# Attention scores in strips of 32 queries, with the mask added by TensorE, and two units to a visit

## The chip, the cores and the metric

One core of one Trainium2 chip. The metric is the device time of one execution in microseconds (us); lower is better. Six engines matter: TensorE (PE in the profile; its weight loads are PEld), VectorE (DVE), ScalarE (ACT), GpSimd (POOL) and SyncE (SP), which issues the transfers. PSUM, where TensorE writes, has eight banks of 2 KB a partition.

## The reference

A windowed attention feeds a maxout FFN. q, k and v are 8 batches x 8 heads x 576 positions x 64, in fp32. The first four heads attend to the last 32 positions (plain), the others to every fourth of the last 128 (dilated).

```python
scores = scale * np.matmul(q, k.transpose(0, 1, 3, 2))
mask_plain = (rel >= 0) & (rel < window)                                  # window = 32
mask_dil = (rel >= 0) & (rel < window * dilation) & (rel % dilation == 0) # dilation = 4
scores = np.where(masks[None, :, :, :], scores, -1000000000.0)
scores = scores - np.max(scores, axis=-1, keepdims=True)
attn = np.exp(scores)
attn = attn / (np.sum(attn, axis=-1, keepdims=True) + 1e-09)
x = np.matmul(attn, v)               # then heads side by side: 4608 tokens x 512
h = np.maximum(np.maximum(x @ w1, x @ w2), x @ w3)    # w1, w2, w3: 512 x 768
return (h @ w_out).astype(np.float32)                 # w_out: 768 x 512
```

## The kernel before

**Units.** Attention is cut into 64 units: 16 halves of 288 positions, times 4 pairs of heads (`half, p = divmod(u, NPAIR)`; pairs 0 and 1 are plain, 2 and 3 dilated). The host lays the dilated heads out by residue, so that their window, too, is 32 neighbouring keys. A plain unit has 3 blocks of 96 queries, each against 128 keys; a dilated one 4 blocks of 72 queries against 104 keys. In either, query i of a block needs the keys from i + 1 to i + 32, counted in the block's keys: a band. The first half of a batch has 32 keys fewer in its first block (plain) or in all (dilated).

**Two ways to do a unit.** Units 0 to 11 (`LEAN`) go through `dense`: TensorE first puts the mask into a bank (identity times `masks`, bf16), adds the scores of both heads, VectorE takes the maxima of a head pair or of one head in one instruction, and TensorE transposes the exponentials. Units 12 to 63 go through `attention` and `behind`, which the change replaces:

- `scores` (line 834): per block and head j one fp32 matmul into `banks[j]`, 96 or 72 queries wide. The two heads use different halves of the array's rows (`kb.t[64j : 64j + 64]`).
- `masked` (line 866): per block and head one `tensor_tensor_reduce` on VectorE; it reads the bank, adds the mask, scales by -0.125, writes into `W` and gives the row minima (`mx`).
- `expo` (line 857): per block and head one ScalarE exponential with the minima as bias; it also gives the row sums (`sm`).
- `clear` (line 892): in first halves GpSimd zeroes the columns of `W` that no key stands for.
- `eps`, `recip` (line 907), `norm` (in the helper `tt`, line 439; VectorE or GpSimd, as the plan decides): the sums become factors, and `W` is multiplied, one instruction a head.
- `turn` (line 928): six VectorE transposes of 32 x 32 squares, for all blocks at once, into `PT`. Only the squares of the band are moved: for query strip i the key strips i and i + 1; the rest of `PT` stays zero.
- `values` (line 940): per block and head an fp32 matmul of `PT` with v into one bank; both heads use different columns of the array. A copy moves it to `raw` (or to `xa`).

**Visits.** TensorE leaves the FFN for one step at a time (`products`): the value products of units whose `PT` is ready, and then scores of later ones. Units 12 to 21 (`TAKEN` = 22) come in pairs, the others one by one, each time with one unit kept in between.

**FFN.** The first 1152 tokens go in three tiles of 384 (`ffn`, lines 1006 and 1059; operands split into a high and a low part, three products). The other 3456 go in four passes of 864, where `combine` prepares sums and differences of token halves (tiles t), `multiplied` multiplies them by prepared weights (line 1306, `wm` from DRAM copies `wS`), and line 1448 multiplies by w_out. In these passes two banks are held for running sums, so that four of the six `b` banks (three couples) are left to attention.

**What sets the order.** Every operation is a step in `Plan`. `deadlines` gives each a due time, back from the FFN, with paces and slacks (`UNIT_PACE`, `UNIT_SLACK`, `COMBINE_SLACK` and others); `order` plays the steps through on a model of the engines and issues them as they come out. Steps with two or three engines in `costs` may move between them. The model's prices and slacks are constants at the top. Before the first FFN step, filler matmuls (line 1551) are put where TensorE would idle. The engines work through their queues in the issued order.

Of the kernel before, what the change touches and what calls it, by code (L numbers as in the profile page):

```python
# [8 lines left out]
F32 = mybir.dt.float32  # L9
# [9 lines left out]
WIN, DIL = 32, 4  # L19
# [10 lines left out]
SHARED = 1.0  # L30
# [5 lines left out]
TAKEN = 22  # L36
# [10 lines left out]
SPILL = 0.065  # L47
MARGIN, MARGIN_FROM = 0.2, 120.0
TO_PE = 0.26
FFN_PACE = 1.044  # L50
UNIT_PACE, UNIT_SLACK, UNIT_LEAD = 1.559, 3.648, 2.329
FILL = 0.22
BURSTS, BURST = (21, 35), 16
WEIGHT_PACE, WEIGHT_SLACK, WEIGHT_LEAD = 0.437, 1.028, 1.545


def blocks_of(hf, dil):

    nb, nq, wk = (4, 72, 104) if dil else (3, 96, 128)
    step, out = (104 if dil else 96), []  # L60
    for i in range(nb):

        mo = WIN if not hf and (dil or i == 0) else 0
        out.append((nq * i, nq, HALF + step * i + mo, wk - mo, mo))
    return out
# [40 lines left out]
class Step:  # L106


    def __init__(self, costs, fn, bufs, nbytes, rows, kind, lead):
# [6 lines left out]
        self.ready = dict.fromkeys(costs, 0.0)  # L116


class Plan:
# [54 lines left out]
    def room(self, st, slots):  # L174
# [6 lines left out]
        for tag in set(new):  # L181
            k = new.count(tag)
            if any(b.width == 2 for b in st.bufs if b.tag == tag and b.slot is None):
                assert k == 1
                at = max(at, self.couple(slots[tag])[0])
            else:
                at = max(at, sorted(slots[tag])[k - 1][0] if len(slots[tag]) >= k else 1e9)
# [11 lines left out]


    def order(self, fill=None):
# [11 lines left out]
        order = []  # L213
        fills, must, bursts = 0, 0, list(BURSTS)
        while len(order) - fills < len(self.steps):
# [43 lines left out]
            for b in st.bufs:  # L259
# [11 lines left out]
            else:  # L271
# [11 lines left out]
                elif e == "dve" and "pool" in st.costs:  # L283
                    both = min(cost, max(0.0, free["pool"] - at))
                    cost += SHARED * both
                    free["pool"] += 0.5 * SHARED * both
                end = free[e] = at + cost
            st.eng = e
# [8 lines left out]
            for n in st.next:  # L297
                n.left -= 1
                for o in n.costs:
                    if e == o:  # L300
                        lat = 0.0 if e == "pe" else 0.03
                    else:
                        lat = self.AFTER[e] + (TO_PE if o == "pe" else 0.0)
                        if n.kind != "ffn" and end > MARGIN_FROM:
                            lat += MARGIN
                    n.ready[o] = max(n.ready[o], end + lat)
# [1305 lines left out]
```

## Time and profile before

| what | value |
|---|---|
| median of 3 runs (lowest to highest) | 741.37 us (740.05 to 741.79) |
| the profiled execution / its span | 739.52 us / 737.7 us |
| granted TensorE clock | full in all slices |
| transfers | 140.16 MB in 83803 packets, 190 GB/s over the span |
| HBM read / written | 113.25 MB / 25.95 MB |

The profile is of one execution. Busy times of engines overlap each other; a matmul's record runs from its start to a modelled end, so that neighbouring records overlap and the distance between starts is the better price. "idle before" is the time an engine stood still ahead of a group, with what released it. `L866` is line 866. A number behind a tile is left out: `banks` stands for all six `b` banks.

### The profile page before, as it was taken

The page shows a single profiled execution, that of the slowest core. Times are in us where ns is not written, and L with a number is a line of the kernel's source. Part 1 is how long each engine was busy: PE and PEld are TensorE (multiplying, and loading weights), DVE is VectorE, ACT ScalarE, POOL GpSimd, SP SyncE. Part 2 cuts the span into 40 slices and gives each one's busy share as a digit, 9 for nine tenths or more (in the row PEclk, how much of TensorE's full clock was granted, in tenths as well). Part 3 has the DMA queues.
Part 4 walks back from the last instruction along what each step waited for, and adds up shares of the span by engine and source line. Part 5 has one row for each costly group of instructions (what it writes and reads, how often), then busy time and mean ns, then how long its engine had stood idle before and what let it go on. Part 6 is the DMA issues. An engine that isn't in the chain of part 4 may idle for free.

```text
span 737.7 us, 14575 instructions
## 1 busy us (share of the span) xinstructions
PE 710.3 (96%) x4880; PEld 612.7 (83%) x4880; DVE 551.2 (75%) x1645; ACT 327.7 (44%) x1136; POOL 314.1 (43%) x388
## 2 busy tenths in 40 slices
PE   7989999989999899999999999999999999999998
PEld 4659888978988788888788899778888877999986
DVE  7988887889878887789867797897788897134241
ACT  4676634424435554445444344545444543222211
POOL 3789457665756411217751122772112185001040
PEclk9999999999999999999999999999999999999999
DMA  9899635246633487876357778435787641677611
GB/s 317 282 340 391 217 103 178 92 144 202 217 113 105 126 239 230 242 232 187 103 170 241 233 228 249 144 113 167 229 239 211 189 131 59 183 223 223 209 43 54
DMA packets 83803, 140.16 MB, mean 190 GB/s; under 512 B 7952, under 2 KB 32272, under 8 KB 83728
## 3 DMA queue, kind: packets, MB, share of 16 engines
q1 hardware_dynamic: 83728, 139.23, 60.5%
q8 instruction: 39, 0.64, 0.4%
q14 instruction: 36, 0.29, 0.1%
HBM read 113.25 MB, written 25.95 MB: 189 GB/s over the span
## 4 chain that ended last, share of the span: by engine, by line
PE 71%; DVE 16%; DMA 5%; POOL 3%; issue 2%; ACT 2%; SPq 0%; DVEq 0%; ACTq 0%; POOLq 0%
PE banks L1306 20%; PE bank L1306 14%; PE bank L1448 14%; PE bank L1006 8%; PE banks L834 5%; DVE PT L928 4%; PE banks L940 4%; DVE tmps L439 3%; DVE W L439 3%; DVE W L866 2%; PE bank L1551 2%; DMA wS<-wu 2%; DVE hx L439 2%; DMA st<-in_w_dn_dram 2%; DMA wS<-tmps 1%
## 5 line engine op out<-in xcount | busy, mean ns | idle before, releaser
L1306 PE MATMUL banks<-t,wm 128*128 128x432 f32 x864 | 188.0, 363 | 3.5 <-DVE mx L866 1.6
L1306 PEld LDWEIGHTS banks<-t,wm 128*128 128x128 f32 x864 | 159.7, 188 | 18.1 <-ACT banks L432 3.0
L857 ACT ACTIVATE W<-W,mx 96x128 f32<-96x128 f32 (+3 forms) x364 | 135.2, 373 | 61.4 <-DVE mx L866 59.6
L1306 PE MATMUL bank<-t,wm 128*128 128x432 f32 x648 | 141.1, 361 | 0.6 <-POOL t L439 0.6
L928 DVE STREAM_TRANSPOSE PT<-W 32x192 f32<-32x192 f32 (+1 forms) x312 | 125.1, 401 | 9.1 <-POOL W L439 3.9
L1306 PEld LDWEIGHTS bank<-t,wm 128*128 128x128 f32 x648 | 120.8, 188 | 8.2 <-POOL t L439 1.0
L1006 PE MATMUL bank<-xa,wu 128*128 128x384 f32 x648 | 119.1, 338 | 2.6 <-ACT xa L432 1.8
L1448 PE MATMUL bank<-wdn,h 128*128 128x512 f32 (+1 forms) x504 | 119.6, 394 | 1.3 <-DVE h L439 0.5
L1006 PEld LDWEIGHTS bank<-xa,wu 128*128 128x128 f32 x648 | 111.5, 188 | 5.8 <-ACT xa L432 2.1
L1448 PEld LDWEIGHTS bank<-wdn,h 128*128 128x128 f32 (+1 forms) x504 | 91.9, 184 | 25.3 <-DVE h L439 1.1
L866 DVE CUSTOM_DVE_ANT_0 W<-banks,masks 96x128 f32<-96x128 f32 (+3 forms) x364 | 76.5, 256 | 38.0 <-PE banks L1306 13.5
L439 POOL TENSOR_TENSOR W<-W,sm 96x384 f32<-96x384 f32 (+4 forms) x56 | 58.5, 1047 | 64.0 <-DVE sm L907 62.5
L902 POOL TENSOR_TENSOR sm<-sm,small_c 96x6 f32<-96x6 f32 (+1 forms) x52 | 14.7, 283 | 134.7 <-ACT W L857 127.7
L857 ACT ACTIVATION_READ_ACCUMULATOR W<-W,mx 72x1 f32 (+1 forms) x364 | 68.6, 188 | 0.0
L432 ACT COPY tmps<-bank 128x432 f32<-128x432 f32 (+1 forms) x47 | 23.7, 504 | 78.1 <-PE bank L1306 63.8
L434 POOL TENSOR_SCALAR h<-hx 128x256 fp32r<-128x256 f32 (+1 forms) x25 | 11.1, 455 | 102.0 <-DVE hx L439 95.9
L439 DVE TENSOR_TENSOR W<-W,sm 96x384 f32<-96x384 f32 (+3 forms) x58 | 53.0, 918 | 1.2
L940 PEld LDWEIGHTS banks<-PT,v 104*64 104x64 f32 (+1 forms) x728 | 28.4, 136 | 21.2 <-DVE mx L866 6.8
L834 PE MATMUL banks<-k 64*96 64x128 f32 (+3 forms) x728 | 44.9, 259 | 0.3
L432 ACT COPY o<-bank 128x512 f32<-128x512 f32 (+1 forms) x34 | 19.9, 584 | 51.6 <-PE bank L1448 44.2
L940 PE MATMUL banks<-PT,v 104*64 104x72 f32 (+1 forms) x728 | 36.5, 241 | 6.4 <-DVE mx L866 3.4
L1059 PE MATMUL bank<-wdn,h 128*128 128x512 f32 x162 | 38.8, 395 | 3.8 <-DVE tmps L439 3.0
(132 smaller groups left out, 908.1 us busy)
## 6 DMA issues: line engine op xcount, KB each, us to landing
wm<-wS SPq DMA_DIRECT2D x252, 256.0 KB
k<-in_qk_d_dram SPq DMA_DIRECT2D x32, 352.0 KB
k<-in_qk_p_dram SPq DMA_DIRECT2D x32, 304.0 KB
wS<-tmps SPq DMA_DIRECT2D x18, 512.0 KB
st<-in_w_up_dram SPq DMA_DIRECT2D x17, 512.0 KB
v<-in_v_d_dram SPq DMA_DIRECT2D x32, 208.0 KB
out_dram<-o SPq DMA_DIRECT2D x25, 256.0 KB
v<-in_v_p_dram SPq DMA_DIRECT2D x32, 192.0 KB
```

Of the source, the lines that this page charges most:

```text
L432: nc.scalar.copy(dst, src)
L439: (nc.vector if eng == "dve" else nc.gpsimd).tensor_tensor(dst, a, b, op=op)
L834: nc.tensor.matmul(banks[j].t[:nq, wk * i : wk * i + nk], kb.t[d, q0 : q0 + nq], kb.t[d, k0 : k0 + nk], start=True, stop=True,)
L857: nc.scalar.activation(a, a, AF.Exp, bias=mx.t[:nq, n : n + 1], scale=-1.0, accum_out=sm.t[:nq, n : n + 1])
L866: nc.vector.tensor_tensor_reduce(W3()[:nq, n, mo : mo + nk], banks[j].t[:nq, wk * i : wk * i + nk], mask[:nq, mo : mo + nk], -0.125, 3e38, ...
L928: nc.vector.transpose(PT.t[c : c + 32, : 2 * nb, 32 * i : 32 * i + 32], W3(e)[32 * i : 32 * i + 32, :, c - e : c - e + 32],)
L940: nc.tensor.matmul(pv.t[64 * j : 64 * j + 64, q0 : q0 + nq], v.t[:wk, j, i, :], PT.t[:wk, nb * j + i, :nq], start=True, stop=True,)
L1006: nc.tensor.matmul(bank.t[:, :n], wu[f].t[:, g, wz, c, :], xa[c].t[:, xz, t0 : t0 + n], start=(m == 0 and c == 0), stop=(m == 2 and c == 3),)
L1059: nc.tensor.matmul(bank.t, hv(hs[f], hz)[:, s0 : s0 + 128], wdn[f].t[:, wz], start=(f == 0 and m == 0), stop=(f == NF - 1 and m == 2),)
L1306: nc.tensor.matmul(bank.t[:, :HP], wv[:, wz, c], t_of(i, xz)[:, c], start=(start and m == 0 and c == 0), stop=(m == 2 and c == 1), skip_gr ...
L1448: nc.tensor.matmul(bank.t[:rows], hz.t[:, f, :rows], wdn[f].t[:, wz], start=(f == 0 and m == 0), stop=(f == NF - 1 and m == 2),)
L1551: nc.tensor.matmul(idle.t, identb, masks.rearrange("p n k -> p (n k)"), start=True, stop=True)
```

## The change

Units 12 to 63 are done in another form; `dense`, the FFN and the transfers keep theirs.

- **Scores in strips.** A block's queries are cut into strips of 32 (dilated: 32, 32 and 8). Strip r needs the keys 32r to 32r + 63 only (dilated, last strip: 40). So a block and head has three matmuls of 32 queries x 64 keys in place of one of 96 x 128. Strip r uses array columns 32r to 32r + 31 and writes the same partitions of its bank; `W` holds 64 columns a block.
- **Mask by TensorE.** Ahead of the scores six bf16 matmuls (3 strips x 2 heads) write the mask, a 32 x 64 band from `strips`, over all blocks of both units. All scores are computed in first halves, too; the mask covers the missing keys, so `clear` and the zeroing of `W` at the start go.
- **Maxima.** One `tensor_reduce` takes the maxima of all blocks and both heads.
- **Exponentials** in two forms by `LATER` = "abbb": every fourth unit subtracts the maxima on VectorE, takes one exponential over the whole unit and sums on VectorE (a); the others scale the maxima by 1/8 (GpSimd or VectorE) and take one exponential a block and head straight from the bank (b).
- **Normalization** is one instruction a unit, over half as many elements as before.
- **Pairs.** `TAKEN` = 70: two units share a couple of banks (`width=2`), one bank a head, and all visits are pairs.
- **The plan.** The model of VectorE and GpSimd sharing a port is finer (`share`, `port`, `grip`), and slacks, paces and prices are new; `MARGIN` goes from 0.2 to 0, `STAGE_H` from 2 to 8, and the forms of the dense units 8 to 11 change.

```diff
-TAKEN = 22
+TAKEN = 70
-FORMS = "adDaaaAaAbDC"
-STAGE, STAGE_H = ["wd", "ss"], 2
-COMBINE_SLACK, PREPARE_SLACK, LOAD_SLACK = 68.535, 38.501, 0.77
-MARGIN, MARGIN_FROM = 0.2, 120.0
+FORMS = "adDaaaAaCADA"
+LATER = "abbb"
+TILE_NS = 14.0
+STAGE, STAGE_H = ["wd", "ss"], 8
+COMBINE_SLACK, PREPARE_SLACK, LOAD_SLACK = 25.759, 134.466, 0.15
+MARGIN, MARGIN_FROM = 0, 120.0
...
+    for j in range(2):
+        d = slice(64 * j, 64 * j + 64)
+        nc.gpsimd.tensor_copy(strips[d], band[d, d].unsqueeze(1).broadcast_to([64, 4, 64]))
+    nc.gpsimd.memset(strips[:, 0, :WIN], NEG)
...
-        banks = [buf("b", f"s{u}_{j}") for j in range(2)]
         def scores():
-            for i, (q0, _, k0, nk, mo) in enumerate(blocks):
+            for r in () if x else range(3):
                 for j in range(2):
                     d = slice(64 * j, 64 * j + 64)
+                    first = int(not hf and r == 0)
+                    if first and not dil:
+                        m = strips[d, :nb].unsqueeze(1).broadcast_to([64, of, nb, 64])
+                    else:
+                        m = strips[d, 1 - first : 2 - first].unsqueeze(1).broadcast_to([64, of, nb, 64])
                     nc.tensor.matmul(
-                        banks[j].t[:nq, wk * i : wk * i + nk],
-                        kb.t[d, q0 : q0 + nq],
-                        kb.t[d, k0 : k0 + nk],
+                        sp.t[32 * r : 32 * r + 32, j, : 64 * nb * of].rearrange("p (x n k) -> p x n k", x=of, k=64),
+                        identb[d, 64 * j : 64 * j + 32],
+                        m,
                         start=True,
-                        stop=True,
+                        stop=False,
+            for n in range(nb):
+                for r in range(3):
+                    rows, nk = min(32, nq - 32 * r), min(64, wk - 32 * r)
+                    q0, k0 = nq * n + 32 * r, HALF + k_step * n + 32 * r
+                    for j in range(2):
+                        d = slice(64 * j, 64 * j + 64)
+                        nc.tensor.matmul(
+                            sp.t[32 * r : 32 * r + rows, j, at + 64 * n : at + 64 * n + nk],
+                            kb.t[d, q0 : q0 + rows],
+                            kb.t[d, k0 : k0 + nk],
+                            start=False,
...
-                def masked(_, n=n, i=i, j=j, nk=nk, mo=mo):
-                    nc.vector.tensor_tensor_reduce(
...
+        t = plan.add({"dve": dve(nw)}, most, [s], [sp, mx])
+        if form == "b":
+            t = plan.add({"pool": 0.22, "dve": 0.165}, eighth, [t], [mx])
...
+                expd.append(plan.add({"act": act(64) + 0.19}, expo_b, [t], [sp, W, mx, sm]))
+        else:
+            t = plan.add({"dve": dve(nw)}, less, [t], [sp, W, mx])
+            t = plan.add({"act": act(nw, False)}, expo, [t], [W])
+            expd = [plan.add({"dve": dve(nw)}, total, [t], [W, sm])]
...
+        t = plan.add({"pool": 0.13 + 0.00188 * nw, "dve": dve(nw)}, norm, [r], [W, sm])
...
+        sp = buf("b", f"s{units[0]}", width=2) if units else None
+        for i, x in enumerate(units):
             plan.lead = UNIT_LEAD * (NPAIR - 1 - x % NPAIR)
-            if x < NPAIR * 2 * B:
-                first, rest, loaded = attention(x, loaded)
-                new.append((x, first, rest))
+            first, rest, loaded = attention(x, loaded, sp, i, len(units))
+            new.append((x, first, rest))
```

How the order of instructions moves is shown at two places. The first is TensorE's queue at a visit in the first pass. Before, in a row (`t`, `wm`: the FFN pass; `PT`, `v`: the value product of one unit; `k`: scores of another, eight matmuls that alternate between two banks, of which two are shown):

```order
L1306 MATMUL banks_96<-t_2708,wm 128x432 x6
L1306 MATMUL bank_102<-t_2673,wm 128x432 x6
L1306 MATMUL bank_103<-t_2673,wm 128x432 x2
L1306 MATMUL bank_103<-t_2674,wm 128x432 x2
L1306 MATMUL bank_103<-t_2673,wm 128x432 x2
L1306 MATMUL banks_98<-t_2706,wm 128x432 x6
L1306 MATMUL banks_96<-t_2674,wm 128x432 x6
L1306 MATMUL bank_103<-t_2684,wm 128x432 x6
L940 MATMUL banks_98<-PT_0_92,v_3572 64x96 x6
L834 MATMUL banks_96<-k_3324 72x104
L834 MATMUL banks_97<-k_3324 72x104
```

Now, at the start of a visit (lines 982, 861 and 875 are the value product, the mask and the scores; `wdn`, `h`: the FFN's second product):

```order
L1491 MATMUL bank_104<-wdn_1126,h_384_4154 128x512 x2
L1491 MATMUL bank_104<-wdn_1126,h_384_4181 128x512
L982 MATMUL banks_99<-PT_0_95,v_4072 64x72 x8
L982 MATMUL banks_99<-PT_1_96,v_4098 64x72 x8
L861 LDWEIGHTS identb
L861 MATMUL banks_98<-strips,identb 32x384
```

and at its end, after the sixth mask matmul:

```order
L861 LDWEIGHTS identb
L861 MATMUL banks_98<-strips,identb 32x384
L875 MATMUL banks_98<-k_3852 32x64 x18
L875 MATMUL banks_98<-k_3892 32x64 x18
L1491 MATMUL bank_103<-wdn_894,h_512_4159 128x512 x2
```

The products of two units stand behind each other, six masks with weights of their own follow, and then 36 (plain) or 48 (dilated) score matmuls of both new units. For units 12 to 63 there were 47 such visits with scores; now there are 26.

The second place is VectorE's queue in a later pass. Before, the end of a unit's masked copies (`ISA` is one copy, the row behind it reads its minima), with the FFN's steps (`hx`, `bank`) between:

```order
L866 ISA W_90,mx_4443<-banks_96,masks 96x128
L866 ISA mx_4443 96x1
L436 COPY banks_96<-bank_103 128x432
L866 ISA W_90,mx_4443<-banks_96,masks 96x128
L866 ISA mx_4443 96x1
L907 RECIPROCAL sm_4426<-sm_4426 96x6
L439 TENSOR_TENSOR hx_2878<-banks_98,hx_2878 128x432
L439 TENSOR_TENSOR W_91<-W_91,sm_4426 96x384
L928 STREAM_TRANSPOSE PT_0_92<-W_91 32x6x32
```

Now, two plain units in the same pass: a pair's maxima (`mx`), the subtraction, sum and normalization of the unit of form a, and the first of its six transposes:

```order
L908 TENSOR_REDUCE mx_4702<-banks_98 96x6
L908 TENSOR_REDUCE mx_4703<-banks_98 96x6
L465 TENSOR_TENSOR W_92<-banks_98,mx_4702 96x384
L465 TENSOR_TENSOR tmps_100<-banks_97,tmps_100 128x432
L465 TENSOR_TENSOR hx_3068<-hx_3068,tmps_100 128x432
L465 TENSOR_TENSOR tmps_101<-banks_97,tmps_100 128x432
L922 TENSOR_REDUCE sm_4807<-W_92 96x6
L465 TENSOR_TENSOR hx_3068<-hx_3068,tmps_101 128x432
L957 RECIPROCAL sm_4807<-sm_4807 96x6
L465 TENSOR_TENSOR W_92<-W_92,sm_4807 96x384
L970 STREAM_TRANSPOSE PT_0_93<-W_92 32x6x32
```

Over the program the 364 masked copies with their 364 reads give way to 52 maxima, 13 subtractions and 13 sums; of the 52 normalizations VectorE does 22 (12 over 384 elements, 10 over 512), and the 312 transposes stay. On TensorE 364 score matmuls become 1092, and 156 mask matmuls come; the value products, the FFN's matmuls and all transfers of data stay in number, and fillers go from 92 to 96.

More of the change, by code (lines that the diff above doesn't have):

```diff
@@ L116, in __init__ @@
         self.ready = dict.fromkeys(costs, 0.0)
+        self.port = "dve" in costs and "pool" in costs
+        self.grip = 0.2 if "act" in costs else 0.5
 class Plan:
@@ L182, in room @@
             k = new.count(tag)
[L183 to L187, printed above, removed]
+            left = slots[tag]
+            for b in st.bufs:
+                if b.tag == tag and b.slot is None and b.width == 2:
+                    t, i = self.couple(left)
+                    left = [x for x in left if not 0 <= x[1] - i < 2]
+                    at, k = max(at, t), k - 1
+            if k:
+                at = max(at, sorted(left)[k - 1][0] if len(left) >= k else 1e9)
         return at
@@ L198, in single, with after, share @@
         return min(free, key=lambda x: (max(x[0], at), x[1] ^ 1 in held, x))
+    def after(self, e, o, n, end):
+        if e == o:
+            return 0.0 if e == "pe" else 0.03
+        lat = self.AFTER[e] + (TO_PE if o == "pe" else 0.0)
+        return lat + (MARGIN if n.kind != "ffn" and end > MARGIN_FROM else 0.0)
+    def share(self, live, until=1e9):
+        live = {e: x for e, x in live.items() if x and x[1] > 1e-6} if until > 1e8 else live
+        left = {e: x[1] for e, x in live.items() if x}
+        ends, t = {}, 0.0
+        while t < until:
+            on = [e for e in left if left[e] > 1e-6]
+            if not on:
+                break
+            k = SHARED * live["pool"][0].grip if len(on) == 2 and live["dve"][0].port else 0.0
+            pace = {"dve": 1 - k, "pool": 1 - 0.25 * k}
+            m = min(until - t, *(left[e] / pace[e] for e in on))
+            t += m
+            for e in on:
+                left[e] -= m * pace[e]
+                ends[e] = t
+        if until < 1e8:
+            for e in left:
+                live[e][1] = left[e]
+        return ends
     def order(self, fill=None):
@@ L282, in order @@
                         tick += 1
[L283 to L286, printed above, removed]
                 end = free[e] = at + cost
+                if e in live:
+                    self.share(live, at - since)
+                    since, live[e] = at, [st, cost]
+                    for o, left in self.share(dict(live)).items():
+                        free[o] = at + left
+                        if o != e:
+                            for n in live[o][0].next:
+                                for x in n.costs:
+                                    n.ready[x] = max(n.ready[x], free[o] + self.after(o, x, n, free[o]))
+                    end = free[e]
             st.eng = e
@@ L299, in order @@
                 for o in n.costs:
[L300 to L306, printed above, removed]
+                    n.ready[o] = max(n.ready[o], end + self.after(e, o, n, end))
                 if not n.left:
@@ L347, in tile_dilated_window_attention__then__maxout_ffn @@
     masks = const.tile([128, 4, 128], BF16, name="masks")
-    mask = masks[:, 1]
+    strips = const.tile([128, 4, 64], BF16, name="strips")
     raw = const.tile([128, 3, NPAIR, HALF], F32, name="raw")
@@ L843, in attention @@
[L843 to L844 removed]
+                        stop=False,
+                        skip_group_check=True,
+                    )
+            for n in range(nb):
[9 more added lines that the diff above has]
+                            start=False,
+                            stop=True,
+                            skip_group_check=True,
+                        )
@@ L1454, in run @@
                     )
-            prev = plan.add({"pe": 0.686}, run, [prev, *part_of[s0, f // 2]], [bank, hi, lo, wdn[f]])
+            prev = plan.add({"pe": 0.69}, run, [prev, *part_of[s0, f // 2]], [bank, hi, lo, wdn[f]])
             if f == NF - 1:
```

151 lines of the change are left out of this document (66 added, 85 removed).

## The prediction

> **What bounds the kernel now.** First the page: its busy table and its slices (tenths of 40 equal slices, with the granted TensorE clock).
>
> ```profile
> PE 710.3 (96%) x4880; PEld 612.7 (83%) x4880; DVE 551.2 (75%) x1645; ACT 327.7 (44%) x1136; POOL 314.1 (43%) x388
> ...
> PE   7989999989999899999999999999999999999998
> ...
> PEclk9999999999999999999999999999999999999999
> ```
>
> TensorE is the bound, at the full clock; no other engine is above 75%. Only two things can therefore move the end: what TensorE has to issue, and the few microseconds in which it waits. The view by stages narrows the place. The columns are TensorE, its weight loads, VectorE, ScalarE and GpSimd, then clock and DMA; 82 us is where the later attention units begin, 247 us where the second kind of FFN begins, and at 612 us the last attention is done.
>
> ```profile
> 82.00:247.00 165.00, 158.05 (x1247) 143.31 (x1246) 138.83 (x464) 72.02 (x287) 100.52 (x110) 1.00 0.44 140
> 247.00:612.00 365.00, 356.69 (x2413) 308.15 (x2411) 299.10 (x997) 174.42 (x662) 134.99 (x176) 1.00 0.66 196
> ```
>
> Of these 530 us TensorE idles 15, and VectorE is busy for 438 (83%): the only engine that can hold TensorE up there. Next the timeline of TensorE around the visits to attention (start, length, group; each visit is a product with the values, L940, then scores, L834). One fp32 matmul shows as two records.
>
> ```profile
> 101.04 1.21 PE L940 MATMUL banks<-PT,v 128*64 128x96 f32 x24
> 102.18 1.65 PE L834 MATMUL banks<-k 64*72 64x104 f32 x32
> 103.76 2.35 PE L1006 MATMUL bank<-xa,wu 128*128 128x384 f32 x12
> ...
> 143.09 1.21 PE L940 MATMUL banks<-PT,v 128*64 128x96 f32 x24
> 144.23 1.26 PE L834 MATMUL banks<-k 64*72 64x72 f32 x32
> 145.42 1.85 PE L1006 MATMUL bank<-xa,wu 128*128 128x384 f32 x9
> ...
> 219.70 0.72 PE L940 MATMUL banks<-PT,v 128*64 128x96 f32 x12
> 220.35 0.74 PE L834 MATMUL banks<-k 64*72 64x72 f32 x16
> 221.02 1.68 PE L1006 MATMUL bank<-xa,wu 128*128 128x384 f32 x8
> ...
> 257.18 2.53 PE L1306 MATMUL bank<-t,wm 128*128 128x432 f32 x12
> 259.55 2.53 PE L1306 MATMUL banks<-t,wm 128*128 128x432 f32 x12
> 262.01 0.72 PE L940 MATMUL banks<-PT,v 128*64 128x96 f32 x12
> 262.65 0.94 PE L834 MATMUL banks<-k 64*72 64x104 f32 x16
> 263.52 1.45 PE L1306 MATMUL bank<-t,wm 128*128 128x432 f32 x6
> 264.80 1.34 PE L1306 MATMUL banks<-t,wm 128*128 128x432 f32 x6
> ...
> 399.38 0.72 PE L940 MATMUL banks<-PT,v 104*64 104x72 f32 x16
> 400.03 0.90 PE L834 MATMUL banks<-k 64*96 64x128 f32 x12
> 400.86 1.45 PE L1306 MATMUL bank<-t,wm 128*128 128x432 f32 x6
> ```
>
> Ends overlap, so I go from start to start. Single visits take 1.32, 1.51 and 1.48 us (219.70 to 221.02, and so on), of which 0.65 is the product; mean 1.44. Around a visit the FFN loses more: 12 undisturbed matmuls take 2.37 (257.18 to 259.55), the 12 before the visit 2.46, and the 6 after it 1.28 instead of half of 2.37: 0.09 + 0.10 = 0.19. **A single visit costs 1.63, two of them 3.25.** Paired visits take 2.72 and 2.33, mean 2.53, so 2.72 with the 0.19.
>
> **The change on TensorE.** Before, units 12 to 21 share 5 visits and units 22 to 63 have 42 of their own; now all 52 share 26. For a pair the product stays at 1.14 (101.04 to 102.18). For scores the price is columns: blocks of 104 columns take 0.87 and of 72 columns 0.67, four blocks each, so 0.20/(4 x 32) = 1.56 ns per column of a block (both heads run together), and 0.67 - 4 x 72 x 1.56 ns = 0.22 of fixed cost. Three blocks of 128 come to 0.82 by this; 399.38's visit shows 0.83. A block is now three strips of up to 64 columns, each for both heads, and six blocks (plain) or eight (dilated) make a pair, on the average seven.
>
> The new thing, six tiles of the array at once, is in no row. Its two halves are: two heads on different rows (L834), and two products on different columns of the array (L940). The latter in a window 20 ns wide:
>
> ```profile
> 262.01 0.30 PE L940 MATMUL banks<-PT,v 128*64 128x96 f32 x2
> ```
>
> Two matmuls start within 20 ns. Lower end: all six run together, a block costs 64 x 1.56 ns = 0.10. Upper end: the three strips run one behind the other, 3 x 0.10 = 0.30 (dilated 0.26, whose last strip has 40 columns). Between them lies a limit by weight loads:
>
> ```profile
> L834 PEld LDWEIGHTS banks<-k 64*72 64x72 f32 x416 | 17.8, 140 | 3.5 <-DVE mx L866 0.7
> L834 PEld LDWEIGHTS banks<-k 64*96 64x96 f32 x312 | 17.4, 160 | 2.1 <-DVE mx L866 0.3
> ```
>
> 24 columns more take 20 ns more, so 32 columns are worth 27; three strips one behind another, twice (two records), are 0.16 a block. But the two tiles of a product, 64 columns each, would by that take 2 x 53 = 0.11 a step, and 399.38 makes eight steps in 0.65, or 0.08. So loads overlap at least in part. I take 0.13, the middle between 0.10 and 0.16.
>
> The mask matmuls are six of 384 or 512 columns in bf16, in the same six tiles. The fillers, from the chain of work, price one:
>
> ```profile
> 12.40 2.48 PE bank L1551 x11
> ```
>
> 11 of 512 columns take 2.48: 0.225 each, all six together thus about 0.22; one strip after the other 0.6, one behind another 1.2.
>
> Sum for a pair: product 1.14 + masks 0.22 + fixed 0.22 + scores 7 x 0.13 = 0.91 + around it 0.19 = 2.68. Against 3.25 that saves 0.57 x 21, against 2.72 it saves 0.04 x 5: **12.2 us**. At 0.10 a pair costs 2.47 and 17.6 us go; at 0.16, 2.89 and 6.7. Strips one after another: 1.14 + 0.6 + 0.22 + 7 x 0.28 + 0.19 = 4.1, which adds 17.9 + 6.9 = 25 us; with the masks singly too, 40.
>
> Two rules of the Trainium skill can be held against this. "TensorE: Matmul & The Clock Gate", in "Wait — 56ns, not 53.3ns?", says that starts of matmuls never come closer than about 25 ns, however few their columns; an estimate by it is 0.30 for the twelve records of a block, and some 19 us lost. The row at 262.01 contradicts it for neighbouring tiles. The same page, "Packing small matmuls — row/col tiling", reports a speedup of 2.38 for three column tiles instead of 3; an estimate from it is 0.126 a block, and the sum by it would be about 13 us. No run here shows that figure.
>
> **The waits.** TensorE's waits by releaser (us in total, times, longest):
>
> ```profile
> PE banks L940 <- DVE mx L866: 3.4, 5, 0.9
> PE bank L1059 <- DVE tmps L439: 3.0, 1, 3.0
> PE banks L940 <- DVE PT L928: 2.7, 5, 1.3
> PE banks L1306 <- DVE mx L866: 1.6, 3, 0.9
> PE banks L1306 <- DVE banks L436: 1.1, 1, 1.1
> ```
>
> Together 11.8 us, all VectorE. Its work for attention, by groups (busy, mean ns of one):
>
> ```profile
> L866 DVE CUSTOM_DVE_ANT_0 W<-banks,masks 96x128 f32<-96x128 f32 (+3 forms) x364 | 76.5, 256 | 38.0 <-PE banks L1306 13.5
> ...
> L439 DVE TENSOR_TENSOR W<-W,sm 96x384 f32<-96x384 f32 x29 | 21.4, 745 | 0.7
> L439 DVE TENSOR_TENSOR W<-W,sm 72x416 f32<-72x416 f32 x15 | 16.1, 1078 | 0.2
> L619 DVE TENSOR_REDUCE mx<-banks 72x4 f32<-72x416 f32 x8 | 4.4, 572 | 0.0
> ...
> 158.60 4.29 DVE L439 TENSOR_TENSOR W<-W,sm 72x288 f32<-72x288 f32 x1
> ...
> 165.79 1.65 PE L1059 MATMUL bank<-wdn,h 128*128 128x512 f32 x6 [3.03 <-DVE tmps L439]
> ```
>
> The 364 masked copies (76.5 us) go. In their place come 52 maxima: 572 ns for 416 elements gives 0.53 for 384 and 0.70 for 512, 32 us in all; the 13 units of form a add a subtraction and a sum of 384, 26 x 0.53 = 14. Normalization keeps half as many elements a unit: on VectorE 12 of 384 and 10 of 512, 8.9 + 13.3 = 22 us, for at least 37.5. So 76.5 + 37.5 - 46 - 22 = 46 us less, and VectorE falls from 83% to 74% of the stretch. The transposes stay, 312 of them. The worst wait, 3.03, came from a normalization that took 4.29 us while GpSimd ran beside it; there are fewer of these.
>
> I count a third of the 11.8, **4 us**, as gained; bounds are 8 us gained and 4 lost, since every placement is new and the plan's margin of 0.2 for late arrivals is now 0. ScalarE is no cover to lose: 364 exponentials become 286 smaller ones and 13 of a whole unit, at 44% busy. GpSimd gets 35 scalings of maxima and loses elements to normalize. The start (weights staged in other buffers, four fillers more, 4 x 0.225, which fill idle time) and the transfers I cost at nothing, since the first FFN tile still needs the same eight units and weights; 2 us either way. After the last product 57 matmuls stand in front of the last pass instead of 72; that cover, 15 x 0.225 = 3.4 us, is not missed as long as the copies behind them are done in 12 us.
>
> Sum: 12.2 + 4 = 16.2. From the profiled execution, 739.52 (span 737.7), that gives 723.3; the median of the runs is 741.37, 1.85 above, and by it **725.2, forecast 725**.
>
> **The rivals.**
> - The pair waits for its later unit (0.20). The product of a visit now stands behind twelve transposes of two units, six of them behind the slower; everything queued on TensorE stands behind it. If each of 26 visits loses 0.5 us, as the five waits on L928 did (2.7/5), that is 13 us, the waits' gain is gone, and it ends at 741.4 - 12.2 + 13 = 742. Against it: visits are some 20 us apart (530/26), twice as far as before.
> - The strips don't overlap (0.14): 25 to 40 us lost, 4 gained, 762 to 777. It decides from 0.22 us a block: then 26 pairs cost (82 + 4)/26 = 3.30, and the change is a loss. For it: no row shows six tiles; against it: each pair of two does overlap.
> - Issue is the limit (0.06). The densest run shown is 16 records in 0.67 - 0.22, or 28 ns a record; a block now has twelve, 0.34. A pair costs 1.14 + 0.22 + 0.22 + 2.38 + 0.19 = 4.15, which adds 18.9 + 7.2, less 4: 764. Against it: those 16 fit their columns, so 28 ns need not be a floor. The 25 ns of the Trainium skill above would be such a floor.
>
> **How the numbers follow.** The forecast has 0.60: a block between 0.10 and 0.16 and waits from 8 gained to 1 lost, 715 to 736. The first rival spreads over 732 to 748. The range 715 to 750 leaves out the two slow ones and little else. A measurement of this kernel tells 0.3% (2.2 us) from no change: below 739.2 lie the forecast and 0.12 of the first rival, faster 0.72; same 0.06; slower 0.22.
>
> **What would show it.** Score groups of a pair should take about 1.1 us from start to start plus 0.2 for the masks, and a visit about 2.5. If scores take over 2, a slow rival is right. L982 (the product's new line) waiting long for transposes at most visits means the first. VectorE should be under 510 us busy in all. The forecast is wrong if TensorE's idle time in 82 to 612 us grows instead of falling, or if the first FFN matmul starts over 2 us later.

## The result: slower by 0.6%, although the part that was meant to get shorter did

| | before | after |
|---|---|---|
| median (lowest to highest, 7 runs each) | 742.72 us (740.05 to 744.32) | 746.69 us (745.91 to 747.87) |
| ratio, 95% interval | | 1.0058 [1.0039, 1.0077] |
| span of the profiled run | 737.7 us | 744.6 us |

The forecast was 725. The profiled execution of before is one of its quicker ones (granted clock 1.00, where most of its runs have 0.992 to 0.998 and 741 to 744 us), so that the two spans lie 6.9 us apart and the medians 4.0. First the page of after, the same three lines as before:

```profile
PE 706.9 (95%) x6492; PEld 602.3 (81%) x6492; DVE 506.9 (68%) x943; ACT 291.3 (39%) x1015; POOL 294.6 (40%) x376
...
PE   8979999999999999999999999899999989999998
...
PEclk9999999999999999999999999999999999999999
```

TensorE is still the bound, but at 95% instead of 96%, with less work and a longer span: it waits more. VectorE lost 44 us of work. The view by stages says where (columns as in the prediction):

```profile
82.00:247.00 165.00, 164.01 (x1832) 149.79 (x1831) 139.39 (x265) 70.92 (x272) 90.74 (x100) 1.00 0.50 161
247.00:612.00 365.00, 345.87 (x3443) 295.66 (x3444) 256.95 (x501) 144.65 (x571) 123.19 (x171) 1.00 0.64 193
```

The first stretch went as hoped: TensorE's idle time fell from 7 us to 1. In the second it rose from 8.3 to 19.1, although VectorE became lighter (257 us busy for 299). TensorE's waits by releaser (us in total, times, longest) name the new one:

```profile
PE banks L1348 <- ACT banks L458: 14.5, 26, 0.6
PE banks L1348 <- DVE banks L462: 3.5, 5, 0.7
PE banks L735 <- ACT banks L529: 3.1, 3, 2.3
...
PE banks L982 <- DVE PT L970: 0.8, 3, 0.4
```

Line 1348 is the pass of the FFN (before: 1306), L458 ScalarE's copy and L462 VectorE's. No attention instruction stands in the two large rows. The same wait is there after 640 us, where no attention is left, and that is the best place to look. Timeline of after (start, length, group, and in brackets the idle time before it and what ended it):

```profile
652.81 2.14 PE L1348 MATMUL bank<-t,wm 128*128 128x432 f32 x10
...
654.78 1.34 PE L1348 MATMUL banks<-t,wm 128*128 128x432 f32 x6
656.16 0.50 ACT L458 COPY banks<-bank 128x432 f32<-128x432 f32 x1 [1.85 <-PE banks L1348]
656.72 1.45 PE L1348 MATMUL banks<-t,wm 128*128 128x432 f32 x6 [0.59 <-ACT banks L458]
...
658.21 0.61 DVE L465 TENSOR_TENSOR hx<-banks,hx 128x432 f32<-128x432 f32 x1 [3.12 <-PE banks L1348]
658.85 0.50 ACT L458 COPY banks<-banks 128x432 f32<-128x432 f32 x1 [2.18 <-DVE hx L465]
...
665.61 0.50 ACT L458 COPY banks<-bank 128x432 f32<-128x432 f32 x1 [1.85 <-PE banks L1348]
```

and the same place of before:

```profile
653.41 2.52 PE L1306 MATMUL bank<-t,wm 128*128 128x432 f32 x12
...
655.76 2.53 PE L1306 MATMUL banks<-t,wm 128*128 128x432 f32 x12
655.97 0.50 ACT L432 COPY banks<-bank 128x432 f32<-128x432 f32 x1 [0.67 <-PE bank L1306]
657.15 0.61 DVE L439 TENSOR_TENSOR hx<-banks,hx 128x432 f32<-128x432 f32 x1 [2.25 <-PE banks L1306]
...
664.24 0.50 ACT L432 COPY banks<-bank 128x432 f32<-128x432 f32 x1 [0.67 <-PE bank L1306]
```

In a weight block (the FFN's work on one block of weights) TensorE makes product 1 in a `bank`, then product 6 of the block before into the second held running sum, then product 2 into the first. Product 2 adds onto product 1, which the copy `banks<-bank` brings into the first sum's bank. Before, that copy starts as soon as product 1 has ended (655.97; 653.41 + 2.52), beside product 6, and TensorE runs twelve matmuls without a gap. After, the copy starts at 656.16, when product 6 (654.78 + 1.34) has ended, and product 2 waits 0.59 for it. From copy to copy a block takes 9.45 us (665.61 - 656.16) instead of 8.27 (664.24 - 655.97), with the same matmuls in the same order.

Product 6 and the copy touch different banks. But in the rows of the order that stand ahead of the prediction, the held sums of before are `banks_96` and `banks_98`, and those of after, in the very same steps, are both `banks_97`:

```
L1348 MATMUL bank_104<-t_2886,wm 128x432 x2
L1348 MATMUL banks_97<-t_2922,wm 128x432 x6
L1348 MATMUL banks_97<-t_2887,wm 128x432 x6
```

`banks_97` is one couple: one PSUM tile of two banks. The change takes whole couples for its pairs of units, and the plan, by its code, keeps couples whole where it can (`single`); that this is why it put the two single banks of the held sums together is read from the code and was not tried by a run. **Theory: waits are kept by tile, so that whatever touches one sum waits for whatever touches the other.** A second wait in each block fits as well. VectorE's reading of the second sum needs product 6 alone. Before, it starts at 657.15, in the middle of the twelve matmuls; after, it starts at 658.21, when product 2 into the other sum has ended (656.72 + 1.45). The copy `banks<-banks` from the first sum to the second stands behind that reading (658.85).

For all runs I split the span by the starts of TensorE's matmuls in the trace: the time to the first FFN matmul; the FFN's matmuls at their undisturbed distance (0.174, 0.229 and 0.196 us for 384, 512 and 432 columns; 561.1 us in every run); visits to attention after that, with the waits in them and what the first distance behind them has above the undisturbed one; and gaps, which is what the other distances of neighbouring FFN matmuls have above those. Some 4 us behind the last matmul make up the span.

| run | start | visits (number) | gaps | span |
|---|---|---|---|---|
| before | 50.3 | 102.3 (57) | 20.0 | 737.7 |
| after | 54.0 | 79.2 (38) | 46.3 | 744.6 |
| e1, after, a tile for each sum | 55.4 | 79.3 (38) | 9.8 | 709.5 |
| e2, before, sums joined | 50.8 | 108.0 (57) | 50.3 | 774.1 |
| e3, after, sums in two couples | 54.9 | 83.3 (38) | 18.2 | 721.5 |
| e4, e1 with the old start | 57.6 | 76.6 (35) | 10.5 | 709.7 |
| e5, before, a tile for each sum | 51.1 | 104.1 (57) | 14.9 | 735.2 |
| e6, e1 with single visits | 54.9 | 96.3 (58) | 23.5 | 739.8 |
| e7, e1 with the old numbers | 53.4 | 78.2 (32) | 16.8 | 713.5 |
| e8, e1 with the heads apart | 54.3 | 84.9 (38) | 8.9 | 713.2 |
| e9, e1 with more on VectorE | 54.8 | 77.2 (37) | 16.3 | 713.4 |
| e10, e1 with less on VectorE | 55.0 | 87.0 (38) | 22.3 | 729.6 |
| e11, e6 with the old numbers | 53.2 | 93.7 (53) | 20.9 | 733.0 |

After gained 23.1 us at the visits and lost 26.3 in gaps and 3.7 at the start.

### The profile page after: what moved, and what is told of

Read it like the earlier page. It is cut to its first block, busy times and chain, and to the rows that moved or that the text cites. A ratio compares the mean times of both kernels' runs of the same rounds, so it can differ in the third digit from the quotient of the medians.

```text
span 744.6 us, 16812 instructions
## 1 busy us (share of the span) xinstructions
PE 706.9 (95%) x6492; PEld 602.3 (81%) x6492; DVE 506.9 (68%) x943; ACT 291.3 (39%) x1015; POOL 294.6 (40%) x376
## 4 chain that ended last, share of the span: by engine, by line
PE 76%; DVE 10%; POOL 5%; ACT 4%; issue 2%; DMA 2%; SPq 0%; POOLq 0%; DVEq 0%; ACTq 0%
PE banks L1348 25%; PE bank L1348 14%; PE bank L1491 11%; PE bank L1048 10%; PE bank L1101 4%; PE banks L982 4%; ACT banks L458 3%; PE banks L875 3%; PE bank L1595 2%; DVE PT L970 2%; DVE h L465 2%; DVE hx L465 2%; DMA wS<-tmps 1%; POOL wu L465 1%; DVE tmps L465 1%
## 5 line engine op out<-in xcount | busy, mean ns | idle before, releaser
L1348 PE MATMUL banks<-t,wm 128*128 128x432 f32 x864 | 195.8, 368 | 20.3 <-ACT banks L458 14.5
L931 ACT ACTIVATE W<-banks,mx 96x64 f32<-96x64 f32 x286 | 85.0, 315 | 30.4 <-PE banks L1348 12.1
L912 POOL TENSOR_SCALAR mx<-mx 96x8 f32<-96x8 f32 (+1 forms) x35 | 8.6, 245 | 139.6 <-DVE mx L908 139.5
L931 ACT ACTIVATION_READ_ACCUMULATOR W<-banks,mx 96x1 f32 x286 | 59.2, 207 | 0.0
L458 ACT COPY tmps<-bank 128x432 f32<-128x432 f32 (+1 forms) x51 | 25.8, 507 | 83.5 <-PE bank L1348 73.8
L465 POOL TENSOR_TENSOR W<-W,sm 96x384 f32<-96x384 f32 (+4 forms) x39 | 40.1, 1031 | 37.0 <-DVE sm L957 33.5
L908 DVE TENSOR_REDUCE mx<-banks 96x6 f32<-96x384 f32 (+1 forms) x52 | 30.0, 614 | 33.2 <-PE banks L875 33.2
L465 DVE TENSOR_TENSOR tmps<-banks,tmps 128x432 f32<-128x432 f32 (+1 forms) x52 | 30.6, 591 | 29.5 <-PE banks L1348 29.3
L465 POOL TENSOR_TENSOR h<-hx,h 128x256 fp32r<-128x256 f32 (+1 forms) x52 | 40.9, 808 | 14.4 <-PE bank L1491 10.9
L952 POOL TENSOR_TENSOR sm<-sm,small_c 96x8 f32<-96x8 f32 (+1 forms) x46 | 12.1, 264 | 83.4 <-ACT W L931 68.1
L458 ACT COPY o<-bank 128x512 f32<-128x512 f32 (+1 forms) x35 | 20.5, 584 | 51.6 <-PE bank L1491 34.2
L465 DVE TENSOR_TENSOR hx<-banks,hx 128x432 f32<-128x432 f32 x24 | 14.5, 606 | 37.6 <-PE banks L1348 37.6
```

The lines of the kernel that those rows point to most:

```text
L458: nc.scalar.copy(dst, src)
L465: (nc.vector if eng == "dve" else nc.gpsimd).tensor_tensor(dst, a, b, op=op)
L908: nc.vector.tensor_reduce(by_row(mx), S4(), axis=mybir.AxisListType.X, op=ALU.max, negate=True)
L931: nc.scalar.activation(W3()[:, m], S4()[:, m // nb, m % nb], AF.Exp, bias=mx.t[:96, m : m + 1], scale=0.125, accum_out=sm.t[:96, m : m + 1],)
L1348: nc.tensor.matmul(bank.t[:, :HP], wv[:, wz, c], t_of(i, xz)[:, c], start=(start and m == 0 and c == 0), stop=(m == 2 and c == 1), skip_gr ...
```

## The experiments

### Is it the tile? e1, e2, e3

e1 keeps the order of after on every engine, row for row. Only when the sums are opened, the couple is given up and taken again as two tiles.

```diff
...
+    whole = tc.tile_pool(name="ps0", bufs=1, space=bass.MemoryType.PSUM)
+    first = whole.__enter__()
-    couples = [ps.tile([128, 2, 512], F32, name=f"banks_{i}", bufs=1) for i in range(3)]
+    couples = [(ps if i else first).tile([128, 2, 512], F32, name=f"banks_{i}", bufs=1) for i in range(3)]
...
             def opened(_):
-                for x in held:
+                whole.__exit__(None, None, None)
+                own = ctx.enter_context(tc.tile_pool(name="ps1", bufs=1, space=bass.MemoryType.PSUM))
+                for i, x in enumerate(held):
+                    x.t = own.tile([128, 512], F32, name=f"lone_{i}", bufs=1)
...
```

> The changed kernel, its order of instructions on every engine kept, but the two held running sums get a tile each (the couple of banks that they shared is given up at the point where they are opened and taken again as two tiles of one bank). Theory (one tile for both sums makes the copy into the first sum's bank, and product 2 behind it, wait for product 6 into the second): TensorE's waits at L1348 for ScalarE's and VectorE's copies (14.5 + 3.5 us after) fall to the few us of before, and the time falls by 17 to 24 us, to 723 to 730. Rival A (the copies are late because the new paces and order put other work ahead of them on ScalarE and VectorE): waits and time stay within 2 us of the changed kernel. Rival B (the strips' units themselves cost TensorE time that the trace books elsewhere): the same, no change.

Measured: **710.16 us (709.78 to 711.24)**, 0.9572 [0.9547, 0.9596] of before and 36.5 us below after. Page, waits and timeline of e1 (the sums are now `lone`, lines moved by 8):

```profile
PE 692.5 (98%) x6492; PEld 608.2 (86%) x6492; DVE 511.3 (72%) x943; ACT 291.0 (41%) x1015; POOL 293.3 (41%) x376
```

```profile
PE bank L1499 <- DVE h L473: 3.0, 2, 1.5
PE bank L1607 <- DVE masks L458: 2.9, 1, 2.9
PE banks L743 <- ACT banks L537: 2.7, 2, 2.3
...
PE banks L990 <- DVE PT L978: 0.8, 3, 0.4
```

```profile
619.23 2.53 PE L1356 MATMUL lone<-t,wm 128*128 128x432 f32 x12
619.43 0.50 ACT L466 COPY lone<-bank 128x432 f32<-128x432 f32 x1 [0.61 <-PE bank L1356]
...
627.51 2.53 PE L1356 MATMUL lone<-t,wm 128*128 128x432 f32 x12
627.71 0.50 ACT L466 COPY lone<-bank 128x432 f32<-128x432 f32 x1 [0.67 <-PE bank L1356]
```

No wait of the pass for a copy is left among the large ones, the twelve matmuls stand in one group again, and the block is back at 8.28 us (627.71 - 619.43). In the traces every engine's instructions come in the same order as in after. With only the tiles cut differently, the cause is shown; rivals A and B, which had left the time as it was, fall. The size I had too small: I had taken it from the view of waits, 18 us. Between neighbouring matmuls of the pass the gaps of after sum to 34.8 us, and in e1 none is above 0.1. Of them 29 are of about 0.75 us, where the view's rows say 0.59; the matmul after each starts another 0.1 late, and the second wait of the block costs 0.1 to 0.3, with 0.1 behind it again.

e2 does the opposite to the kernel before: it forces both sums into one couple (`held0` and `held1` get banks 2 and 3 of six). Scores and masks are as before, and in the trace every engine's instructions come in the same order by line, tile and shape; only the banks differ.

> The kernel before, with the two held running sums forced into the two halves of one couple of banks, which the change had brought about by itself; nothing of the scores or the masks is changed. Theory (shared tile): 18 to 27 us slower than before, 760 to 769, with a wait of some 0.7 us at L1306 for ScalarE's or VectorE's copy in most weight blocks. Rivals A and B (new paces, or the strips): within 3 us of before.

Measured: 775.76 us (773.24 to 775.91), 1.0448 [1.0418, 1.0477]. Waits of e2 (L1312 is the pass):

```profile
PE banks L1312 <- ACT banks L438: 13.6, 23, 0.6
PE banks L946 <- DVE mx L872: 7.7, 11, 0.9
PE banks L1312 <- DVE tmps L445: 5.5, 3, 2.3
```

The same wait for ScalarE's copy appears, nearly as often (23 for 26) and as long as in after, in a kernel without one strip. The time is 7 us above what was expected; visits rose by 5.7 us as well, and the second row was 3.4 before, so part of it is the score banks that moved. One visit, 1.8 us longer, stands at 169 us, where the granted clock was 0.50 (1.00 in before).

e3 is after with `held0` and `held1` forced into banks 0 and 2.

> The changed kernel, with the two held sums forced into halves of two different couples, as they happened to lie before; one whole couple is left for the scores of a pair, and the outputs of attention go to the two spare halves. Theory (shared tile): the waits for the copies go as with tiles of their own, 17 to 24 us; but a pair's scores can no longer be made while the last pair's are read, which may give up to 10 us back: 722 to 738. Rivals A and B: 745 to 750, or slower where the one couple is awaited.

Measured: 723.37 us (722.42 to 724.52), 0.975 [0.9724, 0.9776]. This is within the theory's 722 to 738: the copies' waits go without new tiles. What it lacks to e1 is in the table, 4.0 us at the visits and 8.4 in gaps. Its waits show 4.6 us for ScalarE's `h` at L1497 (the longest 3.4) and one of 3.7 us where the sums are opened. Its order differs from that of after in places, so the clean comparison is e1.

### Where e1's gain over before comes from: e5, e11, e7, e6

e5 gives the kernel before the two tiles of e1 (same edit, banks 2 and 3).

> The kernel before (scores in blocks, mask added by VectorE, one unit a visit late on), with the two held sums in a tile of one bank each, as e1 has them for the changed kernel. It gives the fair base for the change of the scores: before, each held sum shared its couple with a bank of attention. Theory (what the change itself is worth is its visits, 102.3 to 79.2 us of TensorE, and the waits for VectorE that go): own tiles save the kernel before at most 3 us (its stalls behind attention's readers at L1306 are some 2 to 3 us), 739 to 743, and e1 stays 27 to 33 us faster than this. Rival (most of e1's gain over before is the tiles, not the scores): 715 to 725.

Measured: 738.26 us (735.03 to 739.69), 0.9953 [0.9935, 0.9972]; 4.0 us, 1 us more than the theory had said and far from the rival. Before, a held sum shared its couple with a bank of attention, and paid for that: the gaps fall by 5.1. But the 4.0 is what is left beside a loss. In e5's profile one visit waits 5.36 us for its transposes. They stand behind two casts of VectorE that took 6.53 us together, with GpSimd at work beside them; before, the same two took 0.41.

```profile
473.33 6.53 DVE L444 CAST h<-hx 128x192 fp32r<-128x192 f32 x2
482.78 1.23 PE L948 MATMUL banks<-PT,v 104*64 104x72 f32 x16 [5.36 <-DVE PT L936]
```

With the slower clock behind it (0.70 in 483 to 490 us) this visit costs 8.6 us, the same visit of before 1.7, in the same order of instructions. So the tiles may be worth up to some 11 us (an estimate, 4.0 + 6.9), and what e11 gains on e5 says little of the strips alone. Whether e5's other runs have this wait is not known.

e11 has strips and masks, but single visits and all numbers of the plan as before; e7 has pairs as well; e1 has the new numbers too; e6 has these with single visits.

```diff
 e7, on e1:                          and e11, on e7:
-SHARED = 1.2                        -TAKEN = 70
+SHARED = 1.0                        +TAKEN = 22
-FORMS = "adDaaaAaCADA"
+FORMS = "adDaaaAaAbDC"              e6, on e1:
-STAGE, STAGE_H = ["wd", "ss"], 8    -TAKEN = 70
+STAGE, STAGE_H = ["wd", "ss"], 2    +TAKEN = 22
 (and the slacks, paces, leads, SPILL and MARGIN of before)
```

> Strips and masks alone: own tiles for the held sums, the planner's numbers and the single visits from unit 22 on as before, only the scores and what VectorE and ScalarE do with them as in the change. Beside the kernel before with own tiles (738.26 us) it prices the strips by themselves. Theory (a single strip visit is 0.15 to 0.19 us shorter than a single block visit, by the late visits of the runs so far, 1.28 and 1.36 us for 1.46 and 1.51; some 53 visits, with VectorE's load lower, give 8 to 14 us): 724 to 730, so that the single visits' 741.72 us with the new numbers were mostly stalls of a plan whose numbers did not fit. Rival (strips alone are worth nothing; the merging is all): 735 to 743.

> As e1, with all the planner's numbers that the change touched put back (sharing factor, slacks, paces, leads, spill, margin, forms of the early units, staged weights); pairs and strips stay. Theory (the numbers only follow the change; what counts is the visits' price and the tiles): within 6 us of e1, 706 to 717, with stalls of TensorE up where transfers or weights come later. Rival (the numbers hold a good part of the gain): 720 or more.

> As e1 (strips, mask by TensorE, own tiles), but from unit 22 on one unit a visit, as before; a visit then pays the ends of a stretch (0.19 us) and the masks (0.22 us) for one unit. Theory (merging is a saving of its own beside the strips'): some 19 more visits at 0.4 us each, 6 to 10 us above e1: 716 to 720. Rival (the strips do it all, since a pair waits for its later unit): within 2 us of e1, or below it.

| step (each on the one above) | us, median | ratio to before | worth |
|---|---|---|---|
| before | 742.3 | | |
| e5, own tiles | 738.26 | 0.9953 [0.9935, 0.9972] | -4.0 |
| e11, strips and masks | 734.31 | 0.9897 [0.987, 0.9924] | -4.0 |
| e7, pairs | 714.79 | 0.9635 [0.9609, 0.9661] | -19.5 |
| e1, new numbers | 710.16 | 0.9572 [0.9547, 0.9596] | -4.6 |
| after, sums in one tile | 746.69 | 1.0058 [1.0039, 1.0077] | +36.5 |

**In this stack, strips alone give little and pairs most.** e7 kept within its theory (706 to 717). e11 came out between its theory (724 to 730) and its rival (735 to 743), nearer to the rival. By the split its visits are 10.4 us below e5's, but gaps took 6.0 back and the start 2.1. Merging then takes 15.5 us off the visits and 4.1 off the gaps. These steps carry single long waits, too: e5 has the one above, e11 one of 4.3 us for VectorE's `h`, e7 none over 1.5 behind the start. The visits' prices below are free of that. e6 missed its theory by 22 us (741.72 us, 739.73 to 743.74, ratio 1.0 [0.9981, 1.0018]): 17.0 us more at the visits than e1, not 8, and 13.7 more in gaps. Its waits:

```profile
PE bank L1499 <- DVE h L473: 6.8, 3, 4.4
PE banks L990 <- DVE PT L978: 3.9, 2, 3.0
```

Waits of 4.4 and 3.0 us for VectorE stand there; behind the start, e1's longest is 1.5. That numbers made for pairs don't suit single visits is likely (with the old ones, e11 is 7.4 us faster), but which of them was not tried.

Visits from 247 us on, by the starts of their parts (medians over 8 to 18 visits, us):

| (product of plain units / of dilated) | product | masks | scores | together |
|---|---|---|---|---|
| before, single | 0.65 / 0.65 | | 0.87 / 0.81 | 1.51 / 1.46 |
| e6, single | 0.65 / 0.65 | 0.12 / 0.09 | 0.60 / 0.53 | 1.36 / 1.28 |
| e1, pair | 1.14 / 1.15 | 0.23 / 0.17 | 1.07 / 0.90 | 2.44 / 2.23 |

Two single visits of e6 take 2.64, a pair 2.33, and the pair has one set of ends (0.2) instead of two: 0.5 a pair from merging, 0.33 from strips. For the 21 pairs that were single before, that is some 10 and 7 us (estimates), so merging is the larger part, but not nearly all. One visit of each kind, in e1 (pair of plain units) and in e6 (single units):

```profile
344.37 1.32 PE L990 MATMUL banks<-PT,v 104*64 104x72 f32 x32
345.62 0.35 PE L869 MATMUL banks<-strips,identb 64*32 64x384 bf16 x6
345.79 0.97 PE L883 MATMUL banks<-k 64*32 64x64 f32 x72
346.69 1.66 PE L1499 MATMUL bank<-wdn,h 128*128 128x512 f32 x6
```

```profile
341.69 0.72 PE L990 MATMUL banks<-PT,v 104*64 104x72 f32 x16
342.34 0.27 PE L869 MATMUL banks<-strips,identb 64*32 64x192 bf16 x6
342.43 0.60 PE L883 MATMUL banks<-k 64*32 64x64 f32 x36
```

### What a block of strips costs: e8

The strips are issued head by head, so that three tiles of the array stand side by side at a time and not six.

```diff
-            for n in range(nb):
-                for r in range(3):
+            for j in range(2):
+                d = slice(64 * j, 64 * j + 64)
+                for n in range(nb):
+                    for r in range(3):
...
-                    for j in range(2):
```

> As e1, with the same strips in another order: all strips of one head, then all of the other, so that only three tiles of the array (three column groups of one half of the rows) stand side by side at a time instead of six. Theory (strips overlap by tile: a block of six costs what one strip's 64 columns cost, 0.106 us): a block then costs two times that, 0.21 us; 8 plain or dilated blocks to a pair less or more, some 230 blocks of 32 visits add 0.106 each, 20 to 26 us above e1: 731 to 737. Rival (the 12 records of a block are issued at 9 ns each, whatever tile they go to): within 2 us of e1.

Measured: 715.46 us (715.02 to 715.91), 5.3 above e1; neither. The visit of e8 that answers to the one above:

```profile
346.29 0.35 PE L869 MATMUL banks<-strips,identb 64*32 64x384 bf16 x6
346.47 1.15 PE L883 MATMUL banks<-k 64*32 64x64 f32 x72
347.54 1.67 PE L1499 MATMUL bank<-wdn,h 128*128 128x512 f32 x6
```

Six blocks take 1.07 from start to start instead of 0.90. From three to six blocks (e6 and e1) a plain block costs 0.124 us; with the heads apart 0.029 more; a dilated one 0.118 and 0.043 more. So it matters which tiles stand beside each other, against the rival, but three at a time cost 23 to 36% more than six, not twice as much. What limits them was not settled.

### The start, and VectorE's load: e4, e9, e10

e4 puts the start's two constants back on e1 (`FORMS` and `STAGE_H` as in e7's diff).

> As e1, with the two constants that shape the first 50 us put back: the form of each early unit and the number of weights staged at the start (2 for 8). Theory (these two make the first matmul of the FFN start 3.7 us later, 54.0 for 50.3 us): it starts at 50 to 51.5 us, and the time is 2 to 4 us below e1. Rival (the start is longer for the new masks, slacks or sharing factors): within 1 us of e1, start at 53 to 55.

Measured: 712.14 us (711.48 to 712.8), 2.0 above e1, with the first FFN matmul at 57.6 us, later still. Both fail: these constants do not make the late start, and the mark itself was a poor one. e4 has three visits fewer behind its start, 2.7 us less, which was done ahead of it.

e9 and e10 change `LATER` on e1 from "abbb" to "a" and to "b".

> As e1, but every later unit takes the form whose subtraction and row sums are on VectorE; in e1 only each fourth unit does, and the others give them to ScalarE. Theory (TensorE's waits before came with VectorE's 83% load in 82 to 612 us, and e1's drop with its lighter load): some 39 units take two more VectorE instructions of about 0.6 us, so VectorE's busy time there rises from 415 us to some 460 us, above the 447 us of before, and TensorE's stalls between FFN matmuls rise from 7.6 us to 13 to 20 us: 716 to 723. Rival (the waits of before came from shared tiles and the banks' order, not from VectorE's load): within 2 us of e1.

> As e1, but every later unit gives the exponential its maxima and row sums on ScalarE, so VectorE loses some 16 us more in 82 to 612 us and ScalarE gains some 40 us. Theory (VectorE's load carries the waits that are left): 1 to 3 us below e1, 707 to 709. Rival (what waits are left stand elsewhere, and ScalarE's longer exponentials come late): 710 to 714.

Measured: e9 715.25 us (715.17 to 716.12), just below the theory's 716 to 723, e10 733.15 us (729.74 to 735.12). In e9 gaps rose by 6.5 us, about as the theory says, but VectorE's load by much less than it says: 425 us busy in 82 to 612 us (133.12 + 292.29) for 415 in e1 (139.36 + 275.22). The subtractions and sums did add 47 us (61.2 for 14.2), but other work shrank, the FFN's differences in `h` alone from 25.3 us to 13.6, at 782 ns each for 1215. (The 447 us that e9's theory gives for before are 438 by the view.) e10, 23 us above e1, fits neither of its expectations; it has the lighter VectorE of the two and is 18 us slower. Its first waits:

```profile
PE lone L1595 <- ACT W L939: 7.7, 1, 7.7
PE bank L1499 <- POOL h L473: 6.5, 4, 2.0
```

The first is the opening of the sums, which by the row waits until ScalarE has read the scores (`W`); they lay in the couple that the sums take over. So VectorE's load alone doesn't order these kernels; that it carries some of TensorE's waits is neither shown nor refuted.

## Why the prediction was wrong

**The step that failed is "The waits".** It took the list of releasers of before, asked what of it VectorE's relief would save, and set bounds of 8 us gained and 4 lost. The bound on the loss named the new placement and the plan's margin (and the range then used 1 lost, not 4). That placement also means banks, and that the two running sums could come into one tile, it didn't ask, although the quoted rows show it: `banks_96` and `banks_98` in one fence, `banks_97` for every bank that the FFN reads in another. This one term is +36.5 us (e1 beside after), more than the whole change is worth without it. Both signs of being wrong came: TensorE's idle time in 82 to 612 us grew from 15 to 20 us, and the first FFN matmul starts 3.7 us later.

Point by point:

- **The bound.** TensorE at full clock: held, in after (95%) and in e1 (98%).
- **The visits.** Right in mechanism, mis-sized. A pair is 1.15 product + 0.20 masks + 0.98 scores + 0.20 around it = 2.53 (forecast 2.68): by e6 and e1 a block is 0.118 to 0.124 (forecast 0.13), and the fixed cost of the scores 0.13 to 0.16 (forecast 0.22). By the prediction's own sum that is (3.25 - 2.53) x 21 + (2.72 - 2.53) x 5 = 16 us for 12.2. The visits gave 23.1, since the waits in them went too: the two rows on L940, 6.1 us before, are 0.8 now. The sum did not say that merging would be the larger part; e11 and e7 do.
- **The gain in the waits.** With the tiles apart, gaps fall from 20.0 to 9.8, on top of the waits in the visits: well above the 4 us counted, and above the bound of 8. Of this, 5.1 come from the tiles alone (e5).
- **VectorE.** 506.9 us busy (under 510 was the mark) and 396 of 530 us, or 75% (forecast 74%): right, and not what decided.
- **The start at nothing.** 3.7 us later, over its mark of 2; e4 tells that the mark says little about the end. No run settles its cause.
- **The rivals.** A pair that waits for its later unit: no, the waits of L982 for `PT` are 0.8 us in all. Strips one after another, or a limit of issue: no, 96 score records of a pair take 1.07 us. The measured 746.69 lies inside the range of 715 to 750 and near the first rival's 742 all the same; that is chance, since no rival's mechanism is the one that came. Of the two rules of the Trainium skill, both from "TensorE: Matmul & The Clock Gate", the 25 ns floor between starts ("Wait — 56ns, not 53.3ns?") does not hold across these tiles, since twelve records in 0.118 to 0.124 us are some 10 ns each. The estimate of 0.126 a block from the other ("Packing small matmuls — row/col tiling") lies close to what was measured.

Without the shared tile the forecast of 725 would have been too cautious by 15 us, and 710 lies below its range.

## What to carry to other kernels

When a change alters who asks for buffers, compare which tile each long-lived buffer lands in before and after, at places that the change doesn't touch: a new wait in untouched code, ended by an instruction on a different bank, can be a tile held in common. Give accumulators that live through a whole stage a tile each. And price a change as a stack, one part on another: here a gain of 32 us was hidden under a loss of 36, and the largest step of the gain, 19.5 us, came with one constant (`TAKEN`) and not with the part that has the most lines.

## What the hardware showed beside this

- Six tiles of 64 rows by 32 columns do run together. From the timeline of after, eight dilated blocks, 96 records, take 1.07 us from start to start, where the prediction has 0.26 a dilated block for strips one behind the other, 2.1 in all. The six masks of 512 columns take 0.23, as much as one filler of 512 columns (0.225):

```profile
330.83 0.40 PE L861 MATMUL banks<-strips,identb 64*32 64x512 bf16 x6
331.06 1.14 PE L875 MATMUL banks<-k 64*32 64x64 f32 x96
332.13 1.45 PE L1348 MATMUL banks<-t,wm 128*128 128x432 f32 x6
```

- A long wait can cost more than its length. In e6, behind one of 4.44 us, 19 matmuls of 512 columns take 6.87 us, where 11 had taken 2.68, and the granted clock over that stretch is 0.59 (the number ahead of the last two):

```profile
361.79 2.68 PE L1499 MATMUL bank<-wdn,h 128*128 128x512 f32 x11
368.91 6.87 PE L1499 MATMUL bank<-wdn,h 128*128 128x512 f32 x19 [4.44 <-DVE h L473]
```

```profile
368.00:375.00 7.00, 6.09 (x17) 4.81 (x18) 5.79 (x11) 0.53 (x1) 2.32 (x3) 0.59 0.00 0
```

- A wait of 3 us can go either way. In the profiles of before, e5 and e2 TensorE waits 3.03 us at the same matmul for VectorE's `tmps`, some 166 us into the span. In 166 to 170 us the granted clock is then 1.00 in before, 0.57 in e5 and 0.50 in e2.
